# Attention and SoLU kernel on one core: w_out's column sums moved from VectorE to TensorE, w_out and v loaded at other times, and a new written order of all engines

## The chip, the cores and the metric

The kernel runs on one core of a Trainium2 chip. A core has five engines that work beside each other: TensorE (PE, matrix products into PSUM), VectorE (DVE), ScalarE (ACT), GpSimd (POOL) and SyncE (SP), which here issues nearly all DMAs. Each takes its instructions strictly in the order in which they stand in its own queue. The metric is the device time of one execution in microseconds (us).

## What is computed

Clustered attention, and on its output a feed-forward layer with a SoLU activation and a layer norm. Cut to what matters:

```python
def _attn_ref(q, k, v, centroids):        # q, k, v: (4, 8, 768, 64); centroids: (8, 16, 64)
    q_assign = np.argmax(np.einsum('bhsd,hcd->bhsc', q_n, c_n), axis=-1)
    k_assign = np.argmax(np.einsum('bhsd,hcd->bhsc', k_n, c_n), axis=-1)
    mask = q_assign[:, :, :, None] == k_assign[:, :, None, :]
    scores = np.where(mask, scale * np.matmul(q, k.transpose(0, 1, 3, 2)), -1000000000.0)
    ...                                    # softmax over the keys
    return np.matmul(attn, v)

def _moe_ref(x, w_in, w_out, g_ln):       # x: 3072 x 512; w_in: 512 x 1024; w_out: 1024 x 512
    h = x @ w_in
    solu = h * softmax(h)
    ln = (solu - mu) / np.sqrt(var + 1e-06) * g_ln
    return ln @ w_out                     # all float32
```

The layer norm's mean is never taken from the activations. The kernel scales w_out's rows by g_ln and subtracts from each column its mean over all 1024 rows; the product of solu with that centred matrix is the same. So the kernel needs the column sums of g_ln x w_out once, before the first output product, and this is what the change touches.

## The kernel before

**Tiles.** Work runs by batch (4) and pair of heads (4 a batch). q and k of a pair are loaded (`ld`), turned (`tp` on PE for batch 0, kept by `xa`; `xt` on DVE for the others), cast to bf16 (`ca`), and given 16 or 32 extra rows with the one-hot cluster of each token, so that one product makes the score and the mask: `cl` (cluster products on PE), `tb`, `mx`, `oh`, `ot` (DVE), `pl` (placement of the one-hot rows, by POOL, DVE or a DMA) and `bl` (a blank block). v is loaded (`lv`) and cast (`cv`). `S` makes a bank of 512 scores (384 in the first pair), `E` its exponential on ACT, `V` the product with v for 128 queries (six products), `N` the division by the row sum on DVE. There are 294 `S`, 294 `E`, 192 `V` and 39 `N`.

The feed-forward part goes by 24 tiles of 128 tokens: `tx` (x transposed, by DMA but for the last), `h` (hidden product in four parts of two matmuls), `hm` (row maximum, DVE), `ex` (exponential, ACT), `u` (h times the exponential, DVE), `tu` (u transposed), `bn`, `ag` (variance, DVE), `at`, `al` (scale, POOL), `y` (output product in four parts), `sc` (scaling, on ACT or DVE), `ou` (store). h and the sums use three PSUM banks called `hreg`.

**w_in and w_out.** `li0` to `li3` load w_in, `wi0` to `wi3` cast it. `lg`, `gt`, `gk` load g_ln and turn it. `lo0` to `lo3` load w_out, two blocks of 128 rows each, into `w_g`. `su0` to `su7` (lines 568 and 571, DVE) add g_ln x w_g block by block into `w_sum`, 128 x 512. `me` (line 576, PE) multiplies a matrix of 1/1024 with `w_sum`, which sums over the partitions and leaves the column means in `hreg` bank 2. `ce0` to `ce7` (line 579, DVE) write the centred block as bf16. The hidden products of even tiles use banks 0 and 1, of odd tiles banks 1 and 2, so tile 1 can't start before `ce7`.

**Order.** Nothing is scheduled at run time. `Weave.ORDER` has one text per engine: the kinds of operation in the order in which they are issued, `S3` for three score banks in a row. `Weave.AWAY` names single operations that go to another engine than their default. Semaphores are set from the data, so the texts decide what waits behind what. PE takes a new score bank only when one of three PSUM buffers is free, and ACT has nine buffers for exponentials. One PSUM buffer serves the cluster products, the turned g_ln and the outputs in turn.

In PE's order before, the first scores stand behind the transposes of pair 1 (`... cl tp fl5 cl tp2 S3 ...`; `fl` is a product of zeros that only keeps PE busy).

Of the kernel before, what the change touches and what calls it, by code (L numbers as in the profile page):

```python
# [10 lines left out]
F32 = mybir.dt.float32  # L11
# [3 lines left out]
Alu = mybir.AluOpType  # L15
# [7 lines left out]
class Weave:  # L23
# [6 lines left out]
        ld4 lv si ld3 lg ld3 lo ld3 lv ld2 lv lo ld3 lo2 ld5 lv ld3 li4 tx ld lv ld2 tx ld4 lv ld tu  # L30
        ld2 lv ld2 tx ld lv ld3 tu ld3 tu ld3 ou ld4 ou ld tu ld8 ou lv ld2 tu ld5 ou ld2 tx ld tu
        ld4 tx2 ou lv ld3 tu ld6 tu lv ld5 ou ld4 lv tu ld3 pl tu ld ou ld lv ld2 ou pl ld tu ld4 ou
        ld tx tu lv tx pl2 lv pl tx ou2 pl lv tu2 ou pl4 tu tx tu ou tx ou tu2 tx2 ou2 tu tx tu ou
        tu ou tu ou6
    """
    ORDER["POOL"] = """
        po z ca3 pl2 bl cv zo sg pl2 bl z cv pl ca5 pl3 ca2 pl2 cv2 pl3 ca3 cv pl cv pl2 ca pl z cv2
        ca4 z ca wi3 pl2 bl ca pl2 at ca cv2 pl3 ca2 pl ca at al2 z cv2 at cv2 ca al cv pl2 at pl2
        ca2 bl al ca3 pl3 ca2 pl bl ca2 at al cv2 pl3 at pl al bl ca2 pl4 ca bl cv pl at2 pl2 ca al
        bl ca cv ca cv pl al pl2 at cv2 ca2 at pl bl al ca3 cv at ca pl3 al at al cv ca al at ca pl2  # L40
        cv pl bl ca2 bl at ca3 pl bl al2 cv3 at al at4 al2 at al2 at al2 at al at2 al2
    """
    ORDER["PE"] = """
        wm tp2 cp tp cl tp fl5 cl tp2 S3 tp S tp S cq S2 tp S tp S2 cl V3 S2 tp2 S gt V3 S tp S2 tp
        S2 cl S3 V3 S2 tp S3 tp S V3 S3 cl S V S2 V2 S V S5 V2 S2 V2 S2 cl S3 V2 S V2 S4 V2 S2 V2 S4
        V4 S3 me S3 V4 S3 cl S2 V S V2 S2 V S h2 S2 h2 S2 V2 S V2 S2 h V2 h S2 h V S V S2 h S h S2
        V3 S2 h S V3 y2 S2 h S h S2 h S y h S V3 S y V S2 V2 S h cl S3 V h V S2 V2 S h S y4 V S h S
        V S2 h2 y V2 S2 y2 S V y S V2 S2 V cl S3 V h2 S2 y V S y2 S V S V y S V2 S2 cl S2 h S V S V2
        S2 V2 S V S h S2 cl V4 S3 y2 S2 y S V S V S V2 S2 y S V2 S2 h2 V S3 h2 S2 V h y3 h y S V3 S3
        V h2 S2 V cl V S2 h2 S V2 S2 cl S2 V3 S h2 S3 V y S y S2 y V2 h S2 y S V4 h S2 h2 S2 V2 y S  # L50
        y h y V2 S2 h S y S V2 S2 h2 S cl S2 V3 S cl S3 V h S V2 y3 S2 y V S2 V S h3 V2 S2 cl S2 V2
        S y S y3 S V2 S2 V2 S y S2 y S V S V3 S2 y S y S2 V S V h S V2 S2 h2 S h S2 y2 S V2 y h S2 h
        S V3 S3 V h2 y S2 V4 h S h S2 cl S V S h2 S3 V y h y V S h S2 V3 S2 V2 h S3 h2 S2 V3 S y2 V
        S2 h S V2 S h S2 h S h S V3 S V y3 S2 h3 S V2 S2 y V2 S h S y h S2 V S V h2 V S2 y S y2 V S2
        h S V2 S h3 y S2 y2 h S h V2 y S3 h2 S V4 S y3 S h2 V y h2 S V y4 V h2 V y4 h ptx h y4 h2 y3
        h2 y ptu2 y7 ptu2 y5
    """
    ORDER["DVE"] = """
        cn cb ca xa tb mx oh ot pl2 tb mx oh ot pl xa2 cf xa3 tb mx oh ot gk N su2 xa tb mx oh ot
        xa2 xt N tb mx oh ot N xt su2 N su2 tb N su2 mx N oh xt N xt ce ot ce N ce2 tb wi ce3 N hm  # L60
        ce N u mx oh bn ot N hm xt bn u ag bl N bn hm xt bn u ag bn N tb mx bn hm cv oh ot xt ag u
        bn N hm ca xt2 bn N ag tb mx oh xt ot xt u bn2 ca N tb xt mx oh N hm tb ag N ot u xt2 N xt
        mx oh bn2 hm ag N xt u bn ot bn hm tb N u bn2 mx oh ot tb mx hm N ag2 xt2 u oh N hm ot xt u
        bn2 xt bn N bn tb cv hm tb mx oh N ag2 ot u xt bn xt hm tb N u sc N bn xt bn mx N bn oh ag
        ot mx sc bl oh N hm xt ag cv ot u ca2 N hm sc bn2 u tb cv mx hm N bn u ag oh ot bn2 N hm ag
# [103 lines left out]
def kernel(  # L169
# [366 lines left out]
    w_out_c = const.tile([P, n_fc, d_model], BF16, name="w_out_c")  # L536
    w_g = const.tile([P, n_fc, d_model], F32, name="w_g")
# [28 lines left out]
    def sum_w_out(fc):  # L566
        if fc == 0:
            nc.vector.tensor_scalar(w_sum[:], w_g[:, 0, :], scalar1=g_ln2[:, 0:1], scalar2=None,
                                    op0=Alu.mult)
        else:  # L570
            nc.vector.scalar_tensor_tensor(out=w_sum[:], in0=w_g[:, fc, :],
                                           scalar=g_ln2[:, fc:fc + 1], in1=w_sum[:],
                                           op0=Alu.mult, op1=Alu.add)

    def mean_w_out():
        uses(nc.tensor.matmul(hreg[:, 2, :], g_mean[:], w_sum[:]), 2)
# [511 lines left out]
    for f in range(n_f):  # L1088
# [15 lines left out]
        for f2 in range(n_ff2):  # L1104
            for part in range(2):
                nd = [f"tx{fs[0]}"] + [f"wi{dc}" for dc in range(n_dc)]
                if part == 0:
                    bank = at(f, f2)[1]
                    was = f - 1 if f2 else f - 2
                    if was >= 0:  # L1110
                        nd.append(f"u{was}")
                    else:
                        nd += [x for j, x in enumerate(ring_h[-3:], len(ring_h) - 3)
                               if j % 3 == bank]
                        if bank == 2:
                            nd.append(f"ce{n_fc - 1}")
# [74 lines left out]
    for fc in range(n_fc):  # L1191
        add(f"su{fc}", "DVE", 0.78 if fc else 0.5, 30 + fc, (lambda e, fc=fc: sum_w_out(fc)),
            [f"lo{fc // 2}"] + ([f"su{fc - 1}"] if fc else ["gk"]))
# [43 lines left out]
```

## Time and profile before

| | |
|---|---|
| median of 3 runs | 228.96 us (227.82 to 229.19) |
| the profiled execution | 228.71 us |
| its span on the core | 226.5 us |
| granted clock of TensorE | 1.00 in all stages but the last, 0.93 |

| busy, us | PE | DVE | ACT | POOL |
|---|---|---|---|---|
| 0 to 10 us | 7.19 | 5.44 | 4.90 | 4.17 |
| 10 to 20 us | 9.95 | 8.88 | 9.13 | 8.75 |
| 40 to 50 us | 10.00 | 9.48 | 9.53 | 8.91 |
| 90 to 100 us | 8.61 | 8.71 | 9.87 | 4.53 |
| 180 to 190 us | 10.00 | 9.67 | 8.33 | 0.42 |
| 210 to 220 us | 9.96 | 8.91 | 4.40 | 3.30 |

The span is what the profiler sees between the first and the last instruction; the execution's time has 2.2 us more around it. Busy time counts an instruction from its start to its end. Matmuls overlap, so PE's busy time is longer than the time that it adds to the path. In a row of the timeline or of the chain the first number is the start, the second the length, both in us; `x4` counts instructions. A fp32 product shows as two rows, because it is issued as two. The DMA table says how long after its issue a transfer landed.

### The profile page before, as it was taken

How to read it: one execution, taken by the hardware profiler on the slowest of the kernel's cores; microseconds unless marked ns; L12 is line 12 of the kernel's file. 1: busy time of each engine (PE TensorE's matmuls, PEld its weight loads, DVE VectorE, ACT ScalarE, POOL GpSimd, SP SyncE). 2: the span in 40 equal slices, each digit the busy share in tenths (PEclk: the TensorE clock that was granted, in tenths of full speed). 3: DMA queues.
4: the chain of work that ended last, by engine and by line, in shares of the span. 5: the costliest groups of instructions: out<-in, count | busy, mean ns of one | idle time of the engine just before them, and what ended most of it. 6: DMA issues, size and time to landing. Idle time of an engine off the chain costs nothing.

```text
span 226.5 us, 6571 instructions
## 1 busy us (share of the span) xinstructions
PE 216.7 (96%) x2400; PEld 146.3 (65%) x2400; DVE 201.3 (89%) x357; ACT 194.9 (86%) x378; POOL 125.3 (55%) x242
## 2 busy tenths in 40 slices
PE   7799999999999999979999999999999999999993
PEld 3466666667667677756677666787667767665442
DVE  2889999999999999968999999799999997698991
ACT  3699999999999799978989999999989989875352
POOL 3698898965744889605659449316934600410411
PEclk9999999999999999999999999999999999999999
DMA  7998989999999989899989999599942145359522
GB/s 151 337 288 203 266 143 286 258 202 189 156 192 134 228 137 201 165 175 170 204 165 215 166 190 202 120 176 231 169 101 58 21 116 130 58 140 203 170 96 93
DMA packets 126159, 39.10 MB, mean 173 GB/s; under 512 B 115112, under 2 KB 121648, under 8 KB 126128
## 3 DMA queue, kind: packets, MB, share of 16 engines
q1 hardware_dynamic: 124384, 38.16, 81.3%
q10 hardware_dynamic: 1744, 0.52, 1.0%
q8 instruction: 19, 0.31, 0.6%
q14 instruction: 12, 0.10, 0.2%
HBM read 23.11 MB, written 6.29 MB: 130 GB/s over the span
## 4 chain that ended last, share of the span: by engine, by line
PE 73%; DVE 13%; DMA 7%; ACT 3%; issue 3%; SPq 1%; DVEq 0%; ACTq 0%
PE sps L593 22%; PE hreg L702 17%; PE yps L763 15%; PE ops L616 13%; DMA raw<-in_q_dram 4%; PE csc L450 3%; ACT e L599 2%; DVE u L719 2%; DMA xT<-x 2%; DVE nmax L708 2%; DVE cst L459 1%; DVE mx L472 1%; DVE bs L730 1%; DMA raw<-in_k_dram 1%; DVE x L641 1%
## 5 line engine op out<-in xcount | busy, mean ns | idle before, releaser
L599 ACT ACTIVATE e<-sps 128x512 bf16<-128x512 f32 (+1 forms) x294 | 150.0, 601 | 10.5 <-PE sps L593 9.3
L593 PE MATMUL sps<-qk 80*128 80x256 bf16 (+5 forms) x636 | 96.4, 264 | 0.9
L593 PEld LDWEIGHTS <-qk 80*128 80x128 bf16 (+1 forms) x636 | 60.7, 121 | 29.1 <-issue 10.8
L616 PEld LDWEIGHTS <-e 128*128 128x128 bf16 x1152 | 49.4, 97 | 10.1 <-issue 2.1
L616 PE MATMUL ops<-v,e 128*128 128x65 bf16 x1152 | 53.8, 193 | 0.7 <-DVE x L641 0.6
L702 PE MATMUL hreg<-w_in_sb,xT 128*128 128x512 bf16 x192 | 52.8, 379 | 1.5 <-DMA xT<-x 1.4
L763 PE MATMUL yps<-w_out_c,uT 128*128 128x512 bf16 x184 | 48.5, 379 | 0.0
L719 DVE TENSOR_TENSOR u<-e_sb,hreg 128x1024 bf16<-128x1024 bf16 x24 | 29.0, 1207 | 3.6 <-ACT e_sb L714 3.2
L708 DVE TENSOR_REDUCE nmax<-hreg 128x1 f32<-128x1024 f32 x24 | 29.0, 1210 | 3.0 <-PE hreg L702 2.4
L730 DVE BATCH_NORM_STATS2 bs<-u 128x6 f32<-128x512 bf16 x48 | 31.4, 678 | 0.2
L746 POOL TENSOR_SCALAR esq<-es,mv 128x1 f32<-128x1 f32 x24 | 8.5, 354 | 39.8 <-DVE mv L734 22.4
L714 ACT ACTIVATE e_sb<-hreg,nmax 128x1024 bf16<-128x1024 f32 x24 | 26.9, 1120 | 3.2 <-DVE nmax L708 2.6
L514 POOL COPY qk<-oht 32x384 f32<-32x384 f32 (+1 forms) x43 | 22.1, 514 | 12.7 <-DVE oht L494 9.0
L763 PEld LDWEIGHTS <-uT 128*128 128x128 bf16 x200 | 18.2, 97 | 13.1 <-DVE uT L696 1.1
L433 POOL CAST qk<-xt 64x768 bf16<-64x768 f32 (+1 forms) x26 | 22.4, 863 | 4.5 <-DVE xt L393 3.4
L702 PEld LDWEIGHTS <-xT 128*128 128x128 bf16 x192 | 16.6, 97 | 12.4 <-DMA xT<-x 1.6
L435 POOL TENSOR_SCALAR qk<-xt 64x768 bf16<-64x768 f32 (+1 forms) x27 | 23.1, 854 | 1.4
L407 DVE STREAM_TRANSPOSE xt<-raw 128x768 f32<-128x768 f32 x24 | 22.7, 955 | 1.2 <-DMA raw<-in_q_dram 1.0
L641 DVE TENSOR_TENSOR x<-ops,den 128x256 bf16<-128x256 f32 (+1 forms) x39 | 18.9, 486 | 1.3
L740 POOL TENSOR_SCALAR es<-esum 128x1 f32<-128x1 f32 x24 | 5.4, 226 | 24.1 <-ACT e_sb L714 23.5
L532 POOL CAST v<-vf 128x384 bf16<-128x384 f32 x28 | 14.6, 536 | 6.3 <-DMA vf<-in_v_dram 5.8
L778 ACT ACTIVATE y<-yps,alpha 128x512 f32<-128x512 f32 x16 | 11.2, 698 | 6.7 <-PE yps L763 6.5
(78 smaller groups left out, 177.1 us busy)
## 6 DMA issues: line engine op xcount, KB each, us to landing
vf<-in_v_dram SPq DMA_DIRECT2D x16, 384.0 KB, 4.3
out_dram<-y SPq DMA_DIRECT2D x23, 256.0 KB, 2.5
raw<-in_q_dram SPq DMA_DIRECT2D x50, 96.0 KB, 3.6
raw<-in_k_dram SPq DMA_DIRECT2D x50, 96.0 KB, 3.3
w_g<-in_moe_w_out_dram SPq DMA_DIRECT2D x4, 512.0 KB, 6.6
w_st<-in_moe_w_in_dram SPq DMA_DIRECT2D x4, 512.0 KB, 6.6
raw<-in_q_dram SPq DMA_DIRECT2D x3, 384.0 KB, 6.8
raw<-in_k_dram SPq DMA_DIRECT2D x3, 384.0 KB, 6.4
```

The lines of the kernel that those rows point to most:

```text
L407: nc.vector.transpose(xt[:], raws[b, p, i][:].rearrange("p j c -> p (j c)"))
L433: VEC[e].tensor_copy(dst, src)
L435: VEC[e].tensor_scalar(dst, src, scalar1=inv_C, scalar2=1.0, op0=Alu.mult, op1=Alu.mult)
L593: nc.tensor.matmul(sps_[n, k][:, c0:c0 + w], side(b, h // 2, 1, h % 2, keys)[r], side(b, h // 2, 0, h % 2, slice(s0 * P, s0 * P + w))[r])
L599: nc.scalar.activation(es[n, k][:, :w], sps_[n, k][:, :w], Act.Exp, scale=exp_scale, bias=-exp_scale)
L616: nc.tensor.matmul(opss[g][:, s, :VW], es[n, k][:, c0:c0 + P], v1[slot(b, h // 2)][:, h % 2, kt, :VW], start=(kt == 0), stop=(kt == n_t - 1))
L702: uses(nc.tensor.matmul(hreg[:, at(f, f2)[1], :], xTs[f][:, dc, :], w_in_sb[:, dc, f2 * FF2:(f2 + 1) * FF2], start=(dc == 0), stop=(dc == ...
L708: uses(nc.vector.tensor_reduce(ff[f, "nmax"][:], pair_of(f), axis=AXY, op=Alu.max, negate=True), *both(f))
L714: uses(nc.scalar.activation(ff[f, "e"][:], pair_of(f), Act.Exp, bias=ff[f, "nmax"][:], accum_out=ff[f, "esum"][:]), *both(f))
L719: uses(nc.vector.tensor_tensor(ff[f, "u"][:], ff[f, "e"][:], pair_of(f), op=Alu.mult), *both(f))
L730: nc.vector.bn_stats(ff[f, "bs"][:, f2, :], ff[f, "u"][:, f2, :])
L763: ins = nc.tensor.matmul(dst, ff[f, "uT"][:, at(f, f2)[0] * (n_fc // 2) + c, :], w_out_c[:, fc, cols], start=(fc == 0), stop=(fc == n_fc - 1))
```

## The change

w_out's sums become eight fp32 products on PE. g_ln is first spread over 32 columns per block (`gs`, POOL), into a part of `w_out_c` that is free until `ce0`. Then `su0` takes blocks 0 to 3 and `su1` blocks 4 to 7: each block's 32 columns stand on their own quarter of the array and of `hreg` bank 1, and `su1` adds to `su0`. `sk` copies the bank to `w_sum`; each of its 128 rows is a partial sum that stands 32 times, so `me` divides by 32 x 1024.

```diff
+    g_cols = w_out_c[:, 0, :].bitcast(F32).rearrange("p (f c) -> p f c", c=NB)
...
-    def sum_w_out(fc):
-        if fc == 0:
-            nc.vector.tensor_scalar(w_sum[:], w_g[:, 0, :], scalar1=g_ln2[:, 0:1], scalar2=None,
-                                    op0=Alu.mult)
-        else:
-            nc.vector.scalar_tensor_tensor(out=w_sum[:], in0=w_g[:, fc, :],
-                                           scalar=g_ln2[:, fc:fc + 1], in1=w_sum[:],
-                                           op0=Alu.mult, op1=Alu.add)
+    def spread_g():
+        nc.gpsimd.tensor_copy(g_cols, g_ln2[:].unsqueeze(2).to_broadcast([P, n_fc, NB]))
+
+    def sum_w_out(r):
+
+        for c in range(4):
+            fc = 4 * r + c
+            uses(nc.tensor.matmul(hreg[c * NB:(c + 1) * NB, 1, :], g_cols[:, fc, :], w_g[:, fc, :],
+                                  start=(r == 0), stop=(r == n_fc // 4 - 1),
+                                  tile_position=(0, c * NB)), 1)
+
+    def keep_sums(e):
+        src = hreg[:, 1, :]
+        uses(nc.scalar.copy(w_sum[:], src) if e == "ACT" else
+             nc.vector.tensor_copy(w_sum[:], src), 1)
...
-    add("sg", "POOL", 0.2, 20, lambda e: nc.gpsimd.memset(g_mean[:], 1.0 / d_ff))
+    add("sg", "POOL", 0.2, 20, lambda e: nc.gpsimd.memset(g_mean[:], 1.0 / (NB * d_ff)))
...
+    add("gs", "POOL", 0.35, 20, lambda e: spread_g(), ["gk", "wm"])
+    for r in range(n_fc // 4):
+        add(f"su{r}", "PE", 1.06, 30 + r, (lambda e, r=r: sum_w_out(r)),
+            ["gs", f"lo{2 * r}", f"lo{2 * r + 1}"] + ring_free(1),
+            last_tp[-1:] + [f"su{x}" for x in range(r)])
+    add("sk", "DVE", 0.6, 34, keep_sums, [f"su{n_fc // 4 - 1}"], also={"ACT": 0.48})
```

All five texts of `ORDER` and the lists of `AWAY` are new. Their beginnings, where the order differs most for what follows:

```diff
     ORDER["SP"] = """
-        ld4 lv si ld3 lg ld3 lo ld3 lv ld2 lv lo ld3 lo2 ld5 lv ld3 li4 tx ld lv ld2 tx ld4 lv ld tu
+        ld4 lv si ld4 lv lg ld4 lv2 ld4 lo2 ld4 lo ld3 lo ld3 li4 tx ld3 lv3 tx ld4 tu ld9 lv ld tu
...
     ORDER["POOL"] = """
-        po z ca3 pl2 bl cv zo sg pl2 bl z cv pl ca5 pl3 ca2 pl2 cv2 pl3 ca3 cv pl cv pl2 ca pl z cv2
-        ca4 z ca wi3 pl2 bl ca pl2 at ca cv2 pl3 ca2 pl ca at al2 z cv2 at cv2 ca al cv pl2 at pl2
+        po z ca2 pl2 cv z bl pl2 ca z ca pl2 ca z2 ca3 cv ca cv ca pl3 sg ca cv2 pl3 ca2 gs pl ca cv
+        ca wi ca pl2 wi3 bl ca pl2 cv at cv pl ca pl al bl at cv ca pl ca pl cv ca3 al at ca al ca
...
     ORDER["PE"] = """
-        wm tp2 cp tp cl tp fl5 cl tp2 S3 tp S tp S cq S2 tp S tp S2 cl V3 S2 tp2 S gt V3 S tp S2 tp
-        S2 cl S3 V3 S2 tp S3 tp S V3 S3 cl S V S2 V2 S V S5 V2 S2 V2 S2 cl S3 V2 S V2 S4 V2 S2 V2 S4
-        V4 S3 me S3 V4 S3 cl S2 V S V2 S2 V S h2 S2 h2 S2 V2 S V2 S2 h V2 h S2 h V S V S2 h S h S2
+        wm tp2 cp tp cl tp fl5 cl fl4 S3 tp2 S2 tp S cq S tp S2 tp2 S2 V3 S cl S tp2 V3 S gt S tp S
+        tp S2 cl S2 V2 S V S2 tp S2 tp S2 V2 S V S2 cl S2 V2 S V2 S3 V S2 V2 S2 V S cl S3 su S2 V3 S
+        V S3 V3 S2 V2 S V su S2 V S V3 S3 me S3 V4 S3 cl S3 V4 S2 h S h S2 h S h S2 V3 S2 V h S h V S
...
     ORDER["DVE"] = """
-        cn cb ca xa tb mx oh ot pl2 tb mx oh ot pl xa2 cf xa3 tb mx oh ot gk N su2 xa tb mx oh ot
-        xa2 xt N tb mx oh ot N xt su2 N su2 tb N su2 mx N oh xt N xt ce ot ce N ce2 tb wi ce3 N hm
-        ce N u mx oh bn ot N hm xt bn u ag bl N bn hm xt bn u ag bn N tb mx bn hm cv oh ot xt ag u
+        cn cb xa ca tb mx oh ot pl2 tb mx oh ot xa3 bl cf cv xa zo xa2 tb ca mx oh gk N ot tb pl mx
+        xa2 oh xa cv N ot tb pl N xt mx xt N oh ot tb pl2 ca N pl xt mx N sk oh N ot xt ce3 N tb ce5
+        N hm mx N u oh ot bn N bn ag hm xt2 u N bn2 hm ag sc xt u N bn tb hm mx bn oh ag u xt bn ot
...
     ORDER["ACT"] = """
-        wa xa ca xa2 ca3 xa E9 ca E3 xa2 E6 xa E58 ex E11 ex E9 ex E2 sc E9 ex E sc E7 sc E6 ex E5
+        wa xa2 ca2 xa ca2 E12 xa2 E6 xa E58 ex E12 ex E8 ex E8 ex E3 sc E5 ca E2 ex E25 ex E9 sc E6
```

Counted over the whole texts, before and after:

| engine | what changes in number |
|---|---|
| PE | `su` 0 to 2 (four products each), `fl` 5 to 9 |
| DVE | `su` 8 to 0, `sk` 0 to 1, `ca` 6 to 4, `cv` 4 to 5, `bl` 2 to 5, `pl` 3 to 7, `xa` 9 to 10, `zo` 0 to 1, `sc` 8 to 11, `wi` 1 to 0, `tu` 3 to 2 |
| ACT | `ca` 9 to 5, `xa` 7 to 6, `sc` 17 to 14, `tu` 1 to 2 |
| POOL | `ca` 53 to 59, `pl` 55 to 57, `bl` 12 to 9, `cv` 28 to 27, `wi` 3 to 4, `gs` 0 to 1, `zo` 1 to 0 |
| SP | `pl` 10 to 4 |

Ahead of `lo0`, `lo1`, `lo2`, `lo3` stood 10, 15, 18 and 18 `ld`; now 16, 16, 20 and 23. The first real v loads stood behind 13, 15 and 23 `ld`; now behind 8, 12 and 12. `li0` to `li3` and the first `tx` stand behind the same 26 `ld`, 4 `lv` and 4 `lo` as before.

More of the change, by code (lines that the diff above doesn't have):

```diff
@@ L1114 @@
                                if j % 3 == bank]
-                        if bank == 2:
-                            nd.append(f"ce{n_fc - 1}")
+                        if bank:
+                            nd.append(f"ce{n_fc - 1}" if bank == 2 else "sk")
                 af = ([f"h{f}.{f2}.0"] if part else [f"h{f}.0.1"] if f2 else
@@ L1190, with ring_free @@
             also={"DVE": 0.62})
[L1191 to L1195 removed]
+    def ring_free(bank):
+        return [x for j, x in enumerate(ring_h[-3:], len(ring_h) - 3) if j % 3 == bank]
+    add("gs", "POOL", 0.35, 20, lambda e: spread_g(), ["gk", "wm"])
[4 more added lines that the diff above has]
+    add("sk", "DVE", 0.6, 34, keep_sums, [f"su{n_fc // 4 - 1}"], also={"ACT": 0.48})
+    add("me", "PE", 0.9, 36, lambda e: mean_w_out(), ["sk", "sg"] + ring_free(2), last_tp[-1:])
     for fc in range(n_fc):
```

75 lines of the change are left out of this document (37 added, 38 removed).

## The prediction

> **What bounds the kernel now.** I read the head of the page first, then the table of busy time by stages of 10 us, then the chain of waits in order of time.
>
> ```profile
> span 226.5 us, 6571 instructions
> PE 216.7 (96%) x2400; PEld 146.3 (65%) x2400; DVE 201.3 (89%) x357; ACT 194.9 (86%) x378; POOL 125.3 (55%) x242
> ```
>
> ```profile
> 20.00:30.00 10.00, 9.33 (x124) 6.22 (x121) 9.72 (x18) 9.65 (x22) 8.73 (x13) 1.00 0.97 252
> 30.00:40.00 10.00, 9.51 (x141) 6.75 (x138) 9.76 (x19) 9.80 (x21) 8.49 (x13) 1.00 0.87 210
> ```
>
> A stage row gives the stretch, its length, then how long PE, PE's weight loads, DVE, ACT and POOL were busy, the granted clock, the DMA share and GB/s. From 20 to 40 us DVE and ACT each fall short of full by only 0.2 to 0.35 us in ten. A busy PE is no proof of a full one, so I take PE's pace from the chain, where one product follows the other:
>
> ```profile
> 139.85 0.78 PE csc L450 x8
> 146.09 0.44 PE sps L593 x4
> 147.61 0.57 PE ops L616 x18
> 152.27 0.86 PE hreg L702 x4
> 221.31 1.94 PE hreg L763 x16
> ```
>
> That is 0.22 us for a bank of scores (two rows), 0.19 for the six value products of a block, 0.43 for two rows of a hidden product (an output product has the same width), 0.78 for a cluster product. The timeline has the first hidden product here:
>
> ```profile
> 46.52 1.03 PE L702 MATMUL hreg<-w_in_sb,xT 128*128 128x512 bf16 x4
> ```
>
> The written order puts 72 of 294 score banks, 40 of 192 value blocks and 7 of 17 cluster products ahead of it. Behind it remain 222 x 0.22 + 152 x 0.19 + 192 x 0.43 + 10 x 0.78 = 168 us of products, and the last one ends at 221.31 + 1.94 = 223.3, 176.7 us later. So the stage from 46.5 on ("stage two") belongs to PE: under 9 us of it are anything else, the tail included. In the stage before ("stage one", attention alone) PE has room. The same stage table, asked for the score products (first row) and the value products (second), and ACT's timeline:
>
> ```profile
> 35.00:40.00 5.00, 3.39 (x21) 1.81 (x21) 1.00 1.02 282
> 35.00:40.00 5.00, 2.01 (x48) 1.91 (x48) 1.00 1.02 282
> ```
>
> ```profile
> 32.90 16.05 ACT L599 ACTIVATE e<-sps 128x512 bf16<-128x512 f32 x31 [0.16 <-PE sps L593]
> ```
>
> At the pace above PE's work is 21 x 0.11 + 48 x 0.032 = 3.8 of 5 us, while ACT runs 31 exponentials without a gap, 0.52 each. Stage one is ACT's, with DVE just behind.
>
> **The sums.** From the table of groups by line, and the chain:
>
> ```profile
> L571 DVE SCALAR_TENSOR_TENSOR w_sum<-w_g,g_ln,w_sum 128x512 f32<-128x512 f32 x7 | 6.4, 908 | 0.1
> L568 DVE TENSOR_SCALAR w_sum<-w_g,g_ln 128x512 f32<-128x512 f32 x1 | 0.8, 751 | 0.0
> L393 DVE COPY xt<-hreg 128x384 f32<-128x384 f32 x9 | 4.7, 546 | 0.0
> L818 POOL CAST ident_b<-ident_f 128x128 bf16<-128x128 f32 x1 | 0.3, 293 | 0.3 <-DVE ident_f L816 0.3
> ```
>
> ```profile
> 40.29 0.86 PE hreg L576 x2
> ```
>
> Gone from DVE: 6.4 + 0.8 = 7.2 us. New there: one copy out of PSUM, between 0.55 and 0.55 x 512/384 = 0.73; I take 0.6, since part of a copy's time is fixed. New on POOL: the spread of g to 256 elements a partition, between 0.29 (128 elements) and twice that; I take 0.4. POOL has over 1 us in ten free there; without that cover the first of the new products waits for it, and all scores behind. New on PE: eight fp32 products in two groups of four. One fp32 product of this width takes 0.86 (two rows), so eight one after the other would be 6.9 us. But a cluster product is also four fp32 products on four column blocks, 384 wide, and the four take 0.78 together; at 512 that is 1.04 a group. I take 2.1 for both, because form and neighbours are the same. Their cover is PE's room of 1.2 us in five: two groups within nine us fit, with nothing to spare.
>
> The Trainium skill, "TensorEngine Tiling (Array Packing)", Key Properties, says that a change of tiling mode drains the array. If each of the four changes of mode here cost what a run's last product takes beyond the pace (1.03 - 0.86 = 0.17 for the hidden product), the groups would take 2.8 and the sum below would be 0.7 worse, -0.2. The trace doesn't bear it out as an extra: the 0.78 stands in the chain with scores behind it, so its drains are in it.
>
> **What the new order puts back on DVE.** Ahead of the normalisation N6, which releases the first x transpose, DVE gets four more placements, two casts, two v casts, a blank, a clearing and one copy out of PSUM.
>
> ```profile
> L433 DVE CAST qk<-xt 64x768 bf16<-64x768 f32 (+1 forms) x4 | 2.8, 700 | 0.1
> L532 DVE CAST v<-vf 128x384 bf16<-128x384 f32 x4 | 2.0, 505 | 0.0
> L506 POOL COPY qk<-w_out_c 16x384 f32<-16x384 f32 x12 | 7.1, 595 | 1.7 <-DVE w_out_c L491 0.7 <-DVE g_ln L561 0.4
> L431 ACT ACTIVATE qk<-xt 64x768 bf16<-64x768 f32 (+1 forms) x9 | 6.3, 698 | 0.2
> L778 ACT ACTIVATE y<-yps,alpha 128x512 f32<-128x512 f32 x16 | 11.2, 698 | 6.7 <-PE yps L763 6.5
> ```
>
> A placement of this form on DVE isn't in the trace. POOL takes 0.6; DVE may need half of that or as much, and with nothing to choose by I take the middle, 0.45, so 1.8 for four. Casts 1.4, v 1.0, the copy 0.5, blank and clearing together 0.8 (estimated like one placement and a bit), the sums' copy 0.6: 6.1 in all. Net of 7.2, DVE is 1.1 us earlier at N6. ACT gives up four casts and three scalings in all, 7 x 0.7 = 4.9 us, but only a cast and a copy of these (1.2) lie ahead of the first hidden product.
>
> **The start.** Chain, then POOL's timeline:
>
> ```profile
> 9.97 0.56 PE hreg L386 x3
> 11.04 1.65 ACT e L599 x4
> ```
>
> ```profile
> 8.94 0.75 POOL L514 COPY qk<-oht 32x192 f32<-32x192 f32 x2 [0.16 <-DVE oht L494]
> ```
>
> The first scores stood behind pair 1's transposes, which wait for a load that lands at 9.97, although their own placements were done at 8.94 + 0.75 = 9.7. The new order puts the scores first, with four idle products before them. But DVE now does a cast before that clustering's first step (0.4, half the full-size 0.7 and a little), so scores begin near 10.2 and exponentials near 10.5 instead of 11.04. With the 1.2 off ACT, stage one could gain 1.7. Against that stand PE's 2.1, and pair 1's assignment, which DVE now reaches behind blank, v and clearing work.
>
> **The gate of stage two.** SP, POOL and DVE in the timeline, and two rows of the DMA table for single issues (us to landing at the end):
>
> ```profile
> 34.47 2.84 SPq L548 DMA_DIRECT2D w_st<-in_moe_w_in_dram  x4
> 40.45 1.34 SPq L671 DMA_TRANSPOSE xT<-x  x1
> 42.37 3.01 POOL L551 CAST w_in_sb<-w_st 128x1024 bf16<-128x1024 f32 x3
> 45.34 0.65 DVE L551 CAST w_in_sb<-w_st 128x1024 bf16<-128x1024 f32 x1
> ```
>
> ```profile
> w_st<-in_moe_w_in_dram SPq DMA_DIRECT2D x1, 512.0 KB, 6.3
> xT<-x SPq DMA_TRANSPOSE x1, 5.3
> ```
>
> The gate needs the x transpose (40.45 + 5.3 = 45.8) and w_in cast (45.34 + 0.65 = 46.0). The first moves with N6, to 44.7. w_in's loads stand behind the same loads as before, only in another order, so the first lands at 34.47 + 6.3 = 40.8 again, or up to 2 us sooner if small and large pieces mix better. POOL now has all four casts at 1.0 each, and the first of them, waiting for its landing, holds up a q cast and two placements: 40.8 + 1.0 + 0.9 + 1.5 + 3.0 = 47.2, or 45.2. I take 46.2, 0.3 earlier, with 1.3 earlier and 0.7 later as ends.
>
> **What else moves.** Only 70 score banks stand ahead of the gate now: 2 x 0.22 = 0.4 more behind it. And all eight centrings of w_out now precede the first row maximum. Chain, then PE's timeline:
>
> ```profile
> 48.96 1.23 DVE nmax L708
> 50.19 0.67 DVE w_out_c L579
> 50.90 0.60 PE hreg L702 x2
> ```
>
> ```profile
> 99.70 1.04 PE L702 MATMUL hreg<-w_in_sb,xT 128*128 128x512 bf16 x4 [1.39 <-DMA xT<-x]
> ```
>
> So the second tile's hidden product no longer waits at 50.9 for the last centring; I take 0.5 of its 0.67. At 99.7 PE loses 1.39 us to an x transpose that stands on SP behind loads. In the new order it is behind 70 loads again, with one output fewer; I take 0.5. In the tail one copy goes from DVE to ACT, beside other work: 0. SP issues four placements instead of ten; their time there lies beside PE's products: 0.
>
> Sum: -0.3 + 0.4 - 0.5 - 0.5 = -0.9 us. The profiled execution took 228.71 (span 226.5 and 2.2 around it), the runs 227.82 to 229.19 with median 228.96: 228.1 against the median. I count under 1% (2.3 us) as no change, which is about what those runs can tell.
>
> **Rivals.** (a) DVE was the pacemaker and its relief goes through: gate 1.3 sooner, the waits at 50 and 99 gone, half a microsecond of smaller ones: -1.3 + 0.4 - 0.7 - 1.4 - 0.3 = -3.3, 225.7. For it: DVE at 9.7 in ten. Against: behind the gate PE binds. Chance 0.24. The Trainium skill, "SBUF — State Buffer", SBUF: two separate sides, says that a DVE operation with two SBUF inputs and a GpSimd operation that reads SBUF block each other. The sums took 908 ns with two such inputs and 751 with one, which agrees; by it about 1 us of the 7.2 was waiting that passes to DVE's new copies, and (a) would give 226.7.
>
> (b) PE stops for w_out. SP issues its last block now behind 23 loads instead of 18, in the slot that a v load had. The timeline's issue, the DMA table, and w_g's line:
>
> ```profile
> 32.03 0.47 SPq L527 DMA_DIRECT2D vf<-in_v_dram  x1
> vf<-in_v_dram SPq DMA_DIRECT2D x1, 384.0 KB, 4.3
> DMA to landing us min/median/max: 6.2/6.6/8.2
> ```
>
> PE reaches the second group 53 banks in, seven before the mean's product at 40.29: about 40.3 - 7 x 0.52 = 36.6. With v's 4.3 the block lands at 36.3; with w_out's own 8.2 at 40.2, and every score behind it on PE waits, covered only by three score banks for ACT (1.5): 3.6 + 1.0 - 1.5 = 3.1, less the 0.9 above: 231.2. With a late POOL the same stop comes at the first group. It decides over 1% from a landing near 40. Chance 0.16. (c) The new SP order makes two fresh waits of 1.4 in stage two: +1.9, 230.9; chance 0.10. (d) The four blocks don't run side by side: 6.9 - 2.1 = 4.8 more, 232.9; chance 0.02.
>
> **The numbers.** 0.48 for the forecast. Range 225.3 to 231.5: from just under (a) to just over (b), which its upper end needs. Faster than 226.7: (a) and a little of the forecast, 0.26. Slower than 231.2: (d), half of (b), some of (c), and the forecast's waits that I could not see, 0.25.
>
> **What would show it.** Two groups of about 1.0 us on PE between 30 and 38 us; the first exponential near 10.5; no wait for w_g; first hidden product near 46, with no centring ahead of the second. A w_in cast that ends past 47, or PE waiting for w_g, would turn it; an x transpose waited for again in stage two would leave no gain.

## The result and the profile after

The changed kernel takes 225.82 us (median of 6 runs, 225.53 to 226.4) where the kernel before takes 228.56 in the same comparison (6 runs, 227.82 to 230.3). The ratio is 0.9872, with a 95% interval from 0.9842 to 0.9902: 1.3% faster, or 2.9 us (2.7 between the medians). The forecast was 228.1 with a range of 225.3 to 231.5. The range held the time, but the gain is three times the 0.9 us of the sum, and almost exactly what rival (a) gave, 225.7. The range reaches so low only because of (a), whose mechanism the experiments refute, so that it held is luck.

The head of the page after:

```profile
span 223.9 us, 6574 instructions
PE 215.1 (96%) x2388; PEld 148.1 (66%) x2420; DVE 197.3 (88%) x359; ACT 191.5 (86%) x371; POOL 127.1 (57%) x247
PE 86%; ACT 5%; DVE 3%; issue 3%; DMA 1%; POOL 1%; ACTq 0%; DVEq 0%; POOLq 0%
```

The third line gives each engine's share of the chain of waits. The chain now runs through PE for 86% of the span, and hardly touches DVE or a DMA. The first stage, from the chain (PE), and the timeline (the other engines):

```profile
31.91 0.99 PE hreg L574 x8
36.98 1.00 PE hreg L574 x8
```

```profile
10.52 3.56 ACT L607 ACTIVATE e<-sps 128x384 bf16<-128x384 f32 x9 [1.11 <-PE sps L601]
14.80 1.25 ACT L607 ACTIVATE e<-sps 128x384 bf16<-128x384 f32 x3 [0.72 <-PE ops L624]
38.04 0.69 DVE L581 COPY w_sum<-hreg 128x512 f32<-128x512 f32 x1 [0.34 <-PE hreg L574]
29.34 0.39 POOL L568 COPY w_out_c<-g_ln 128x256 f32<-128x256 f32 x1
42.57 3.00 POOL L552 CAST w_in_sb<-w_st 128x1024 bf16<-128x1024 f32 x3
46.16 0.60 PE L710 MATMUL hreg<-w_in_sb,xT 128*128 128x512 bf16 x2
```

Nearly every price of the prediction stands there: the two groups of sums took 0.99 and 1.00 (1.04 was taken), the copy out of PSUM 0.69 (0.6), the spread 0.39 (0.4). The first exponential starts at 10.52, w_in's last cast ends at 45.57, and the first hidden product starts at 46.16 instead of 46.52, 0.36 sooner (0.3 was forecast). That much is also the scatter between executions: with the same order up to there the first hidden product came at 46.5 and 46.6 in two more traces, and with before's at 46.5 to 47.4 in three more. PE waits for no w_out block. So up to the gate the change does what was said, in size too. The 2.9 us must be made later. The x transpose that PE waited for at 99.7 shows one place. SP's timeline before, then after:

```profile
91.65 2.04 SPq L399 DMA_DIRECT2D raw<-in_q_dram  x2
93.78 0.47 SPq L790 DMA_DIRECT2D out_dram<-y  x1
94.30 1.11 SPq L399 DMA_DIRECT2D raw<-in_q_dram  x2
95.50 1.44 SPq L671 DMA_TRANSPOSE xT<-x  x1
```

```profile
93.04 1.24 SPq L679 DMA_TRANSPOSE xT<-x  x1
```

In both kernels the normalisation that this transpose needs, N17, ends at 93.00 (the next two fences, before and after). Before, SP was then still at a load, with one more load, an output and two loads in front of the transpose, each 0.4 to 0.6 us to issue; after, the transpose leaves at once, 2.5 us earlier, and PE's wait is gone.

```profile
92.58 0.42 DVE L641 TENSOR_TENSOR x<-ops,den 128x256 bf16<-128x256 f32 x1
```

```profile
92.58 0.42 DVE L649 TENSOR_TENSOR x<-ops,den 128x256 bf16<-128x256 f32 x1
```

Two tables worked out from the traces carry the rest. The first is ACT's track: when the n-th of the 294 exponentials starts, against the kernel before (negative is earlier; the time before in brackets).

| exponential | 1 (11.04) | 25 (22.61) | 43 (32.02) | 46 (33.87) | 55 (38.25) | 70 (46.13) | 85 (55.37) |
|---|---|---|---|---|---|---|---|
| after | -0.52 | +0.04 | +0.05 | -0.05 | +0.64 | +0.58 | -0.06 |
| start_only | -0.97 | -0.08 | -0.06 | -0.05 | -0.07 | -0.05 | -0.05 |
| sums_only | -0.38 | -0.38 | -0.57 | +0.28 | +1.18 | +1.13 | +1.13 |

A row's first number also holds where that execution happened to start (10.1 to 10.9 in the traces with the new opening, 10.7 to 11.5 with the old one); what counts is how it moves from there. The start's half microsecond is used up by the 25th exponential, the groups of sums put the track 0.6 behind, and at 55 us, nine microseconds into stage two, both kernels are level: nothing at all has been gained by then.

The second table counts what PE loses from there on. For the row maximum of tile f I take its start on DVE, and subtract PE's work that is written ahead of it, at the paces of the prediction (0.22 a score bank, 0.19 a value block, 0.43 two rows of a hidden or output product, 0.78 a cluster product). How much this difference grows is time in which PE did no such work. (At tiles 7 and 23 the row maximum starts about 0.1 us behind its hidden product, at tile 1 0.6 to 0.8, so a figure is good to about 0.2.) The column "xT late" is the time from the end of N17 to the issue of the x transpose shown above. Each row is one execution, and its time can lie over 1 us from the median of its kernel.

| kernel | stage one | stage two | xT late | lost, tiles 1 to 7 (55 to 107 us) | lost, tiles 7 to 23 (to 215 us) |
|---|---|---|---|---|---|
| before | old | old | 2.5 | 2.2 | 3.3 |
| after | new | new | 0.0 | 0.1 | 2.6 |
| h1 | new | old | 0.8 | 0.4 | 4.7 |
| h2 | old | new | 0.0 | 0.3 | 2.8 |
| sums_only | old, sums on PE | old | 0.9 | 0.8 | 4.1 |
| start_only | old, new start | old | 2.6 | 1.8 | 3.1 |
| n18_first | old | old, one move | 3.1 | 2.8 | 3.3 |
| three_n | old | old, three moves | 2.8 | 2.4 | 4.8 |
| sums_back, sums_late | new, sums on DVE | new | 0.0, 0.0 | 0.1, 0.1 | 2.7, 2.8 |
| late_gate, early_gate | new | new | 0.0, 0.0 | 0.1, 0.1 | 2.6, 2.6 |
| after_sp_old | new | new, SP old | 0.7 | 1.2 | 2.5 |
| ab_h8 | new | new to tile 8, then old | 0.0 | 0.1 | 4.0 |

Before and after differ by 2.8 us here, as much as the whole gain. And the losses go with the written order of stage two, whatever stage one was: 0.1 to 0.3 and 2.6 to 2.8 with the new one, 0.4 to 2.8 and 3.1 to 4.8 with the old one. In before, 1.9 of the 2.2 fall on tile 6, whose hidden products need that x transpose (0.2 in after). With the old order tile 6 loses 1.5 to 2.4 where the transpose left over 2 us late and 0.2 to 0.4 where it left under 1 us late: the old order loses there what SP's queue happens to cost in that execution. Medians and ratios below leave out four executions that took over 1.5% longer than the fastest of the same kernel.

### The profile page after: what moved, and what is told of

Same layout as the page of the kernel before. It is cut to its first block, busy times and chain, and to the rows that moved or that the text cites. A ratio compares the mean times of both kernels' runs of the same rounds, so it can differ in the third digit from the quotient of the medians.

```text
span 223.9 us, 6574 instructions
## 1 busy us (share of the span) xinstructions
PE 215.1 (96%) x2388; PEld 148.1 (66%) x2420; DVE 197.3 (88%) x359; ACT 191.5 (86%) x371; POOL 127.1 (57%) x247
## 4 chain that ended last, share of the span: by engine, by line
PE 86%; ACT 5%; DVE 3%; issue 3%; DMA 1%; POOL 1%; ACTq 0%; DVEq 0%; POOLq 0%
PE sps L601 28%; PE hreg L710 18%; PE yps L771 16%; PE ops L624 14%; ACT e L607 5%; PE csc L450 4%; PE hreg L386 2%; PE hreg L574 1%; PE hreg L771 1%; DMA c_all<-in_centroids_dram 1%; PE csc L445 1%; DVE bs L738 1%; DVE u L727 1%; ACT xt L393 0%; PE hreg L584 0%
## 5 line engine op out<-in xcount | busy, mean ns | idle before, releaser
L601 PE MATMUL sps<-qk 80*128 80x256 bf16 (+5 forms) x636 | 93.8, 264 | 1.8 <-POOL qk L514 0.7
L624 PEld LDWEIGHTS <-e 128*128 128x128 bf16 x1152 | 50.4, 97 | 12.3 <-issue 1.9
L624 PE MATMUL ops<-v,e 128*128 128x65 bf16 x1152 | 55.0, 193 | 0.1
L710 PE MATMUL hreg<-w_in_sb,xT 128*128 128x512 bf16 x173 | 49.1, 379 | 1.1
L771 PE MATMUL yps<-w_out_c,uT 128*128 128x512 bf16 x171 | 46.4, 379 | 0.6
L514 POOL COPY qk<-oht 32x384 f32<-32x384 f32 (+1 forms) x50 | 24.4, 488 | 15.8 <-DVE oht L494 13.6
L433 POOL CAST qk<-xt 64x768 bf16<-64x768 f32 (+1 forms) x31 | 26.1, 842 | 5.5 <-DVE xt L393 3.9
L757 POOL TENSOR_TENSOR alpha<-esq,halves 128x1 f32<-128x1 f32 x24 | 13.5, 561 | 2.0
L786 ACT ACTIVATE y<-yps,alpha 128x512 f32<-128x512 f32 x13 | 9.0, 692 | 6.4 <-PE yps L771 6.0
```

Of the source, the lines that this page charges most:

```text
L433: VEC[e].tensor_copy(dst, src)
L514: ins = VEC[e].tensor_copy(dst.bitcast(F32), src.bitcast(F32).unsqueeze(1) .to_broadcast([NB, 2, n // 2]))
L601: nc.tensor.matmul(sps_[n, k][:, c0:c0 + w], side(b, h // 2, 1, h % 2, keys)[r], side(b, h // 2, 0, h % 2, slice(s0 * P, s0 * P + w))[r])
L624: nc.tensor.matmul(opss[g][:, s, :VW], es[n, k][:, c0:c0 + P], v1[slot(b, h // 2)][:, h % 2, kt, :VW], start=(kt == 0), stop=(kt == n_t - 1))
L710: uses(nc.tensor.matmul(hreg[:, at(f, f2)[1], :], xTs[f][:, dc, :], w_in_sb[:, dc, f2 * FF2:(f2 + 1) * FF2], start=(dc == 0), stop=(dc == ...
L771: ins = nc.tensor.matmul(dst, ff[f, "uT"][:, at(f, f2)[0] * (n_fc // 2) + c, :], w_out_c[:, fc, cols], start=(fc == 0), stop=(fc == n_fc - 1))
```

## The experiments

All were timed against the kernel before on the same chip (medians of before 229.0 to 229.1 in the three sets). Their edits are moves in the written order, shown by the names of operations.

**First set: the sums or the order?** Two theories: R, that DVE's relief by the sums carries through, and O, that the new order makes the gain.

sums_only takes before's order with the sums alone moved:

```diff
-DVE: su0 su1 su2 su3 su4 su5 su6 su7
+POOL: pl0.3.1.1 gs
+PE: S10.1 su0 S10.2
+PE: S13.1 su1 S13.2
+DVE: N5 sk
```

> The order of before with the sums alone moved to PE (the spread on POOL, two groups on PE, one copy on DVE; no load and nothing else moves). Kernel before 228.6, changed kernel 225.8. Theory R (the relief of DVE, 7.2 us less 0.7, carries through into the second stage): most of the gain is here, 226.0 to 226.8, with the first hidden product up to 1 us earlier and the waits for DVE at 110 to 117 and 163 to 168 us gone or smaller. Theory O (the new written order makes the gain, the sums' move by itself is worth little): 228.0 to 229.0, and the stretches at 90 to 100, 110 to 117 and 163 to 168 us leave PE as before.

Measured: 230.24 us (11 runs), ratio 1.0054 (1.0018 to 1.0091): 1.2 us slower. ACT's timeline in this kernel:

```profile
33.66 4.51 ACT L612 ACTIVATE e<-sps 128x512 bf16<-128x512 f32 x9 [0.72 <-PE sps L606]
38.93 9.44 ACT L612 ACTIVATE e<-sps 128x512 bf16<-128x512 f32 x18 [0.76 <-PE sps L606]
```

After each group ACT stands 0.7 us for scores, and by the track the two groups cost 0.85 and 0.89, most of their 2.0 us on PE. In the old order the relief of DVE brings nothing before the gate. R falls.

sums_back takes the changed kernel with the sums back on DVE:

```diff
-POOL: gs
-PE: su0 su1
-DVE: sk
+DVE: N0 su0 su1
+DVE: su2 su3 N3 su4 su5
+DVE: N4 su6 su7
```

> The changed kernel with the sums back on DVE as eight operations (two after the first normalisation, two ahead of the fourth, two behind it, two after the fifth), and without the spread, the PE groups and the copy; the loads and the rest of the order stay. Theory R: most of the gain is lost, 227.6 to 228.6, with exponentials of stage one waiting for DVE's assignments, and the first hidden product about 1 to 2 us later. Theory O: 225.6 to 226.6, since PE gets 2.0 us back in stage one and DVE's 6.5 lie beside ACT's work.

Measured: 240.03 us (6 runs), ratio 1.0503 (1.0451 to 1.0555). Neither theory expected that. DVE's timeline:

```profile
24.38 0.49 DVE L572 TENSOR_SCALAR w_sum<-w_g,g_ln 128x512 f32<-128x512 f32 x1 [6.01 <-DMA w_g<-in_moe_w_out_dram]
```

The sums stood where w_out, loaded later in the new order, had not landed, and DVE waited 6.0 us with all that is behind them; PE's granted clock was 0.50 from 26 to 30 us and from 45 to 50 us. That prices a badly placed wait, not the sums, so sums_late (below) repeats it with the blocks landed.

h1 is the changed kernel up to the first hidden product and before's order from there; h2 the reverse:

```diff
 ORDER, AWAY up to the first hidden product: of one kernel
-ORDER, AWAY from there: of the same kernel
+ORDER, AWAY from there: of the other kernel
```

> The changed kernel up to the first hidden product (all engines, sums on PE included), and from there the written order and the engines of before. Theory R: 225.6 to 226.6, because stage two inherits DVE's lead. Theory O, with the gain in stage two's order: 228.0 to 229.0, with PE waiting again at about 99 us for an x transpose (1.4) and at 110 to 117 for DVE.

> The kernel before up to the first hidden product (sums on DVE), and from there the written order and the engines of the changed kernel. Theory R: 228.0 to 229.0, DVE being late in stage two as before. Theory O: 225.6 to 226.6, with PE without waits over 1 us between 52 and 215 us.

Measured: h1 228.05 (12 runs), ratio 0.996 (0.9924 to 0.9996); h2 226.73 (12 runs), ratio 0.991 (0.9874 to 0.9946). The order of stage two alone, with the sums still on DVE, gives 2.1 of the 2.9 us; the new stage one alone 0.9, with a wide interval. O holds (h2 lies 0.1 above its range). In its trace h1 is 0.5 late at 55 us and gains at 90 to 105 us, where the x transpose left 0.8 late instead of 2.5; sums_only, with the old stage one, shows the same, so whether h1's 0.9 belongs to stage one is open. The moved loads of w_out and v were not tried alone; h2, which has the old ones, lacks 0.9 of the gain, and its interval overlaps that of after.

**Second set: which waits, and what the gate costs.** I read the chain of before as if normalisation N18 on DVE released the x transpose of 95.5, and moved it:

```diff
-DVE: u5 xt2.2.0 xt2.2.1 N18
+DVE: u5 N18 xt2.2.0 xt2.2.1
```

> The kernel before with one move on DVE: normalisation N18, which releases an x transpose, ahead of the two token transposes that wait for a load (raw of k) at 92.9 us. Theory O1 (the largest single piece of stage two's gain is this wait: DVE stands for a load in front of N18, the x transpose is issued at 95.5 and PE waits for it at 99.7; the load's landing varies, and with it the time of before, 227.5 to 230.7 in 29 runs): 227.2 to 228.0 in median, 1.1 to 1.9 under before, with runs closer together, PE without a wait over 0.5 us from 90 to 105. Theory O2 (the whole order is needed, no single wait decides): under 0.5 faster.

Measured: 228.94 (12 runs), ratio 0.9996 (0.9971 to 1.002): nothing, as O2 has it. PE's timeline in it:

```profile
95.16 1.04 PE L768 MATMUL yps<-w_out_c,uT 128*128 128x512 bf16 x4 [1.16 <-DMA uT<-u]
101.11 0.81 PE L707 MATMUL hreg<-w_in_sb,xT 128*128 128x512 bf16 x3 [0.47 <-DMA xT<-x]
```

My reading was wrong: in before N18 ends at 96.86, after that transpose had left. It needs N17, which ended at 93.00, and stood behind loads on SP, as the rows further up show. So this run does not test whether that wait is the largest piece; in n18_first the transpose left 3.1 us late, and tile 6 lost 2.4. The traces of before and after say that in the profiled executions it is: 1.7 of 2.8.

three_n moves two more normalisations, for which value products on PE wait:

```diff
-DVE: hm8 N21
+DVE: N21 hm8
-DVE: cv3.3.0 mx3.3 hm14 N30
+DVE: N30 cv3.3.0 mx3.3 hm14
```

> As n18_first, and two more normalisations moved on DVE: N21 ahead of the row maximum of tile 8 (PE's values wait for it at 118.1 us) and N30 ahead of a v cast, an assignment maximum and the row maximum of tile 14 (PE's values wait for it at 168.0). Theory O1: 226.0 to 227.2, nearly all of stage two's gain by three moves. Theory O2: within 0.5 of n18_first, or slower, since each row maximum moved back holds up its own tile's exponential and the hidden products behind it.

Measured: 231.04 (9 runs), ratio 1.0089 (1.0054 to 1.0125): 2.0 slower. DVE's timeline in it:

```profile
166.82 0.20 DVE L633 RECIPROCAL den<-ops 128x6 f32<-128x6 f32 x1 [1.49 <-PE ops L621]
168.25 1.22 DVE L713 TENSOR_REDUCE nmax<-hreg 128x1 f32<-128x1024 f32 x1
```

The moved N30 asks for value products that PE has not reached. DVE stands 1.5 us in front of it, and the row maximum behind it, which the hidden products need, is 2 us later. An early place for one operation is no gain while PE's order is the old one.

late_gate puts two score banks of the changed kernel ahead of its first hidden product again:

```diff
-PE: S19.0 h0.0.0 S19.1 h0.0.1 S19.2 S20.0
+PE: S19.0 S19.1 S19.2 h0.0.0 h0.0.1 S20.0
```

> The changed kernel with two score banks moved back ahead of the first hidden product on PE, 72 as in the kernel before; nothing else moves. By the prediction's term (two banks more behind the gate cost 2 x 0.22): 0.4 faster, 225.4. Theory G (ahead of the gate a bank goes at ACT's pace, 0.52; behind it at PE's 0.22, so the earlier gate gained 2 x (0.52 - 0.22) = 0.6): 0.6 slower, 226.4, with the first hidden product about 1.0 later, at 47.2.

Measured: 226.31 (10 runs), ratio 0.9909 (0.988 to 0.9939): 0.5 slower than after by the medians, 0.85 by the ratios. The intervals overlap, but the sign is that of theory G, and the trace says the same: between the 70th and the 85th exponential it falls back 0.5 us against after. The traced execution, at 227.76, lost another 1.6 us far ahead of the edit, where a token transpose on DVE waited 1.6 us for a late load of k, and its first hidden product came at 48.39; so with the new order, too, executions differ (226.0 to 228.6 in these ten).

sums_late repeats sums_back with each w_out block landed:

```diff
+DVE: N2 su0 su1
+DVE: N3 su2 su3
+DVE: N4 su4 su5
+DVE: N5 su6 su7
```

> The changed kernel with the sums back on DVE, two of the eight operations behind each of the third to sixth normalisations, so that each w_out block has landed when DVE comes to it; no spread, no PE groups, no copy. Theory R2 (the new order of stage one needs the 6.5 us of DVE that the sums gave up, and would otherwise be late at the gate): first hidden product 1.5 to 5 us later, 227 to 231. Theory S (the two groups cost about 1.0 us of exponentials in stage one and DVE's relief is worth nothing there): 224.8 to 225.6, faster than the changed kernel.

Measured: 232.92 (5 runs), ratio 1.0144 (1.0094 to 1.0194): 6 to 7 us slower than after, more than even R2 has. Theory S falls. The first hidden product comes at 52.97, 6.8 late, and from there on the kernel loses hardly more than after does (the second table). PE's timeline, and the table by stages (PE's busy time is the third number, the granted clock the third from the end):

```profile
36.89 0.60 PE L597 MATMUL sps<-qk 80*128 80x256 bf16 x4 [1.32 <-DVE qk L510]
41.38 0.61 PE L597 MATMUL sps<-qk 80*128 80x256 bf16 x2 [2.29 <-DVE qk L510]
```

```profile
35.00:40.00 5.00, 2.13 (x34) 1.29 (x31) 4.84 (x8) 3.06 (x6) 4.74 (x6) 1.00 0.99 355
42.00:44.00 2.00, 2.00 (x20) 1.44 (x18) 1.94 (x5) 1.76 (x4) 0.00 (x0) 0.50 0.00 0
48.00:50.00 2.00, 1.94 (x35) 1.65 (x34) 1.89 (x3) 1.61 (x4) 2.00 (x3) 1.00 0.95 160
```

DVE, busy 4.84 of 5 us, brings the placements late, PE starves, and its clock is halved on top. By the 52nd exponential, at 42.1 us, the kernel is 5.1 behind after; the other 1.7 come by the 60th, at 48.4, in the stretch of half clock. So DVE's relief is needed in the new stage one, as far as these two placements of the sums show: the new order has filled DVE with other work (placements, casts). It is spent there, not carried on.

**Third set: the pieces.** after_sp_old gives SP alone its old order from the first hidden product on:

```diff
-SP, from h0 on: relative order of after
+SP, from h0 on: relative order of before
```

> The changed kernel with SP's queue alone, from the first hidden product on, in the relative order of before (two placements more on SP stay where they are). Theory D (stage two's gain is in when loads, x and u transposes are issued: PE's waits for a transpose at 85 to 105 us come back): 227.0 to 228.5. Theory W (it is in the orders of PE, DVE and ACT): 225.5 to 226.3.

Measured: 226.51 (6 runs), ratio 0.9893 (0.9859 to 0.9928): 0.5 to 0.7 over after, between the theories, and the intervals overlap. In its trace, an execution of 227.32, the x transpose again leaves behind two loads on SP, 0.7 after N17, but the hidden products that need it (98.64) do not wait. SP's timeline, then PE's:

```profile
93.98 1.10 SPq L404 DMA_DIRECT2D raw<-in_q_dram  x2
95.19 1.35 SPq L684 DMA_TRANSPOSE xT<-x  x1
```

```profile
69.57 1.04 PE L776 MATMUL yps<-w_out_c,uT 128*128 128x512 bf16 x4 [0.54 <-DMA uT<-u]
92.02 0.54 PE L629 MATMUL ops<-v,e 128*128 128x65 bf16 x12 [0.23 <-DVE x L654]
98.64 1.04 PE L715 MATMUL hreg<-w_in_sb,xT 128*128 128x512 bf16 x4
```

PE loses 1.2 instead of 0.1 up to tile 7, and beyond that the same 2.5 as after. It loses them at 69.57 to a u transpose, and at 92.02 to a normalisation that stood on DVE behind a token transpose, which waited 0.6 for a load of q. So in this execution the loss of SP's old order comes through other transfers than the x transpose.

ab_h8 goes back to before's order at tile 8:

```diff
 ORDER, AWAY up to h8.0.0: of after
-ORDER, AWAY from there: of after
+ORDER, AWAY from there: of before
```

> The changed kernel up to the first hidden product of tile 8 (about 110 us), and from there the order and the engines of before. Theory F (stage two's gain, 2.1 us in the run with before's first stage, is made ahead of 110 us): 225.8 to 226.5. Theory L (it is made in the second half, at the values that wait for a normalisation): 227.3 to 228.3. Half each: 226.8.

Measured: 227.54 (8 runs), ratio 0.9938 (0.9912 to 0.9963): 1.5 us over after by the ratios. That lies inside L's range, but it is half of the gain, the other half being made ahead of 110 us. PE's timeline in it:

```profile
166.44 0.36 PE L630 MATMUL ops<-v,e 128*128 128x65 bf16 x6 [0.31 <-DVE x L655]
201.29 1.04 PE L716 MATMUL hreg<-w_in_sb,xT 128*128 128x512 bf16 x4 [0.57 <-DMA xT<-x]
```

The waits of the old order come back: its losses grow by 0.6 at tiles 8 and 9 (0.3 in after), 1.0 at tiles 14 and 15 (0.2) and 0.8 at tile 21 (0.2).

start_only makes the scores of before start first:

```diff
-PE: cl0.0.1 tp0.1.0.0 tp0.1.0.1 S0.0 S0.1 S0.2
+PE: cl0.0.1 S0.0 S0.1 S0.2 tp0.1.0.0 tp0.1.0.1
-ACT: xa0.1.0.0 E0.0 E0.1 E0.2
+ACT: E0.0 E0.1 E0.2 xa0.1.0.0
```

> The kernel before with the first three score banks ahead of pair 1's transposes on PE, and pair 1's copy behind three exponentials on ACT; nothing else moves. By the prediction's start term alone, 0.5 faster: 228.6 against 229.1, with the first exponential at 10.5 and the first hidden product at 46.0. Theory N (ACT gives the half microsecond back before 25 us, where it waits for assignments, as in the changed kernel): within 0.2 of before.

Measured: 228.75 (12 runs), ratio 0.999 (0.9959 to 1.0021): 0.2 under before, as theory N has it, though the interval would hold 0.5 as well. The trace decides: its first exponentials come 0.97 sooner, and the seventh is back at before's time:

```profile
10.07 1.25 ACT L604 ACTIVATE e<-sps 128x384 bf16<-128x384 f32 x3 [0.49 <-PE sps L598]
12.50 2.02 ACT L604 ACTIVATE e<-sps 128x384 bf16<-128x384 f32 x5 [0.41 <-PE sps L598]
```

early_gate was meant to beat both kernels:

```diff
-PE: V17.1 S18.2 S19.0 h0.0.0 S19.1 h0.0.1 S19.2 S20.0 h0.1.0 S20.1 h0.1.1
+PE: V17.1 h0.0.0 S18.2 h0.0.1 S19.0 S19.1 h0.1.0 S19.2 h0.1.1 S20.0 S20.1
```

> The changed kernel with the first tile's hidden products two, two, one and one score banks earlier on PE (first of them behind V17.1, at about 45.7 us, when the x transpose and w_in's last cast have just landed). Theory G (a bank ahead of the gate costs ACT's 0.52, behind it PE's 0.22): 225.2 to 225.5, faster than both kernels. If the gate's inputs are late by then: 225.8 or slower, with PE waiting at 45.7 for xT or for the cast.

Measured: 226.31 (6 runs), ratio 0.9875 (0.9844 to 0.9905), no better than after. The inputs were there; but with hidden products in front of scores ACT ran dry, as its timeline shows, and it fell back 0.5 us between the 67th and the 85th exponential:

```profile
47.03 4.24 ACT L611 ACTIVATE e<-sps 128x512 bf16<-128x512 f32 x8 [0.27 <-PE sps L605]
```

So an earlier gate than the new order's gained nothing. No kernel of these beat the changed one.

## Why the prediction was right and wrong

**What bounds the kernel.** Right: stage one is ACT's with DVE just behind, stage two PE's. Wrong was that PE has room in stage one (see the sums), and what I drew for stage two. "Under 9 us of it are anything else" was read as little to gain, and only two of those waits (49 and 99 us) went into the sum. The value products behind a late normalisation were left out, though before's chain passes through DVE from 109.7 to 117.9 and from 163 to 168. Its ends there:

```profile
117.91 0.21 DVE mv L734
118.14 0.54 PE ops L616 x12
167.39 0.57 DVE x L641
168.00 0.36 PE ops L616 x6
```

This is the error of the forecast: beyond 55 us its sum had 0.5, for the x transpose, and the traces of before and after differ there by 2.8. The second half of stage two, taken at nothing, brought 1.5 us in ab_h8 (0.7 between the traces of before and after). The terms ahead of 55 us, -0.3, +0.4 and -0.5, came to -0.06 on ACT's track.

**The sums.** Sizes right. The cover, "two groups within nine us fit", failed: ACT stands for scores behind each group, so PE's spare 1.2 us in five do not cover a block of 1.0 at once. In the old order they cost 1.2 us of the whole, on ACT's track 1.7; in the new one the track slips by about 0.4 at the first group and 0.5 at the second. The rule on drains at a change of mode, from the Trainium skill, "TensorEngine Tiling (Array Packing)", Key Properties, adds nothing here: groups of 0.99 and 1.00 with scores right behind leave no room for extra drains.

**The start.** -0.5 came at the first exponential and was worth nothing: in both orders ACT waits for scores and values before 25 us, and in after as in start_only the lead is gone by then.

**The gate.** -0.3 forecast, -0.36 measured, but for another reason: the 70th exponential is 0.6 later than before, and the gate is earlier because two banks fewer stand ahead of it. The size is no more than the scatter given above.

**Two banks more behind the gate.** +0.4 has the wrong sign. Ahead of the gate a bank costs ACT's 0.52, behind it PE's 0.22; late_gate, which undoes it, falls back 0.5 in its trace and is slower by about as much, though the intervals overlap.

**The centrings.** The wait for the last one is gone. Of the 0.65 that ACT's track gains between the exponentials 70 and 85, the gate explains 0.5, so 0.15 is left where I took 0.5. No run tried it alone.

**The x transpose.** Right mechanism: it stood behind loads on SP. The size was wrong: I took 0.5 because it is again behind 70 loads, but in the new order SP reaches it before N17 is done. In the profiled executions that is worth 1.7 (tile 6 loses 1.9 before and 0.2 after), and little in executions where the old order's SP is early. SP's old order as a whole costs 0.5 to 0.7 in the median.

**The rivals.** (a) hit the number and fell as a mechanism: sums_only has the relief and is slower, and the gate did not come 1.3 sooner. In its weighing of the shared port, 908 against 751 ns said nothing, since the two operations differ alone, too (0.75 and 0.49, last section). (b) did not happen, w_out landed in time for PE; sums_back shows what a wait for it costs. (c): no wait of PE above 0.4 appeared in stage two after. (d): the blocks run side by side.

Why the whole order works where single moves fail can only be argued: N30 helps only if PE reaches the values earlier too. The order of PE, DVE or ACT alone was not tried beside the old order of the others. What the old order loses at 85 to 105 us differs much between executions, and goes with how late the x transpose leaves (0.8 to 3.1 us); why SP comes to it sooner in some executions is open. Before's times spread from 227.5 to 230.7 in 29 runs. After's six lie within 0.9, but late_gate's ten, with nearly the same order, within 2.6.

## What to carry to other kernels

List every wait on the chain in the stage where the bounding engine ought to be alone, and price them all: that is what a new order can win, and moving one operation, as in n18_first and three_n, can hand its wait to a neighbour or miss it. Relief of an engine is worth nothing by itself in a stage that another engine paces; it is worth something only if the time is spent on work that had been late. A start that is earlier on one engine must be followed down that engine's track until it is used or lost.

## What the runs showed of the hardware

**The clock fell after gaps shorter than 3 us.** In sums_late PE's longest gap was 2.29 us, with 1.32 and 0.64 shortly before, and the granted clock went to 0.50 (0.93 from 40 to 41 us, 0.50 from 41 to 47). The chain of waits of that kernel, the same six score products at half and at full clock:

```profile
42.31 1.28 PE sps L597 x6
48.08 0.67 PE sps L597 x6
```

The Trainium skill, "TensorE: Matmul & The Clock Gate", Why this matters for your kernels, asks for no idle gaps above about 3 us between bursts of matmuls. The half clock agrees with the trace; the limit was too generous here, where PE was busy 2.13 of 5 us and never idle for 3.

**DVE and POOL stop each other.** In sums_back a pair of the same operation on DVE took 0.75 each while POOL stood idle (until 42.53), and a later pair 1.49 each while POOL cast without a gap; POOL's cast of 64x768 took 1.15 there and 0.82 at 34.63. The slow pair fell into a stretch of half clock on PE, but that is not the reason: in sums_late a pair takes 2.98 at full clock (37.98, POOL casting) and one 1.53 at half clock (43.23, POOL idle). DVE's timeline in sums_back, then in sums_late, then POOL's in sums_back:

```profile
37.42 1.50 DVE L575 SCALAR_TENSOR_TENSOR w_sum<-w_g,g_ln,w_sum 128x512 f32<-128x512 f32 x2
45.39 2.98 DVE L575 SCALAR_TENSOR_TENSOR w_sum<-w_g,g_ln,w_sum 128x512 f32<-128x512 f32 x2
```

```profile
37.98 2.98 DVE L575 SCALAR_TENSOR_TENSOR w_sum<-w_g,g_ln,w_sum 128x512 f32<-128x512 f32 x2
43.23 1.53 DVE L575 SCALAR_TENSOR_TENSOR w_sum<-w_g,g_ln,w_sum 128x512 f32<-128x512 f32 x2
```

```profile
42.53 0.50 POOL L510 COPY qk<-w_out_c 16x384 f32<-16x384 f32 x1 [6.17 <-DVE w_out_c L495]
44.46 1.15 POOL L437 CAST qk<-xt 64x768 bf16<-64x768 f32 x1
45.56 1.03 POOL L555 CAST w_in_sb<-w_st 128x1024 bf16<-128x1024 f32 x1
46.57 1.26 POOL L439 TENSOR_SCALAR qk<-xt 64x768 bf16<-64x768 f32 x1
```

That is the rule which the prediction weighed, from the Trainium skill, "SBUF — State Buffer", SBUF: two separate sides: a DVE operation with two inputs in SBUF and a POOL operation that reads SBUF hold one port in turn. The trace agrees: an operation held up in this way took twice its time. At 0.75 for seven of them and 0.49 for the first, the sums alone are 5.7 us, so about 1.4 of before's 7.1 was waiting; the prediction took 1.
